# A new order for the first list of steps of a sparse-attention and gated-MLP kernel

## The chip, the cores and the metric

The kernel runs on one core of one Trainium2 chip. The metric is device time in microseconds for one execution, taken as the median of several runs. The kernel before takes 561.27 us (three runs, 560.92 to 561.34).

## The reference

Eight batches of 576 tokens. Each has eight heads of sparse attention: heads 0 to 3 look back within 32 tokens, heads 4 to 7 at the tokens of the same residue modulo 32. The heads' outputs, side by side, go through a gated MLP with a layer norm over half of its features, a mixing of tokens by `w_sg`, a projection and a residual. `w_in` and `w_out` come in float64.

```python
scores = scale * np.matmul(q, k.transpose(0, 1, 3, 2))
mask_local = (rel >= 0) & (rel < stride)
mask_strided = (rel >= 0) & (pos[None, :] % stride == pos[:, None] % stride)
...
attn = np.exp(scores)
attn = attn / (np.sum(attn, axis=-1, keepdims=True) + 1e-09)
return np.matmul(attn, v).astype(np.float32)
...
h = x @ w_in
h = 0.5 * h * (1.0 + np.tanh(c * (h + 0.044715 * h ** 3)))
u, v = (h[..., :d_ff // 2], h[..., d_ff // 2:])
v_n = (v - mu) / np.sqrt(var + 1e-06) * g_ln
v_s = np.einsum('ts,bsd->btd', w_sg, v_n) + b_sg[None, :, None]
return (x + (u * v_s) @ w_out).astype(np.float32)
```

## The kernel before

The work of a batch is cut into steps of one or a few instructions: a load (`qk_rows`, `v_load`), a block of matmuls (`local_scores`, `strided_pv`, `v_mm`, `u_mm`, `sg_mm`, `out_mm`), a softmax part (`sm_mask`, `sm_max`, `sm_sub`, `sm_exp`, `sm_sum`, `sm_mul`), a layer-norm part, a store. The table `STEPS` (line 978) gives each a short name, and four strings of such names, `START`, `SECOND`, `LATER` with `CYCLE`, and `LAST`, say in which order they are issued. `START` (line 25) is issued once, ahead of everything else: it holds all of the attention of batch 0, the attention of batch 1, the MLP of batch 0, and the preparation of the weights. The lists behind it go batch by batch, the attention of one batch woven into the MLP of the one before.

A word reads so: the name; `-` for the batch at hand, no sign for the next one (names in lower case: the batch at hand), `+` for the one after, `=` for a step of no batch; `^` sets a flag (line 1011) that moves the step to another place: with it `slow()` is VectorE instead of GpSimd, `fast()` is GpSimd instead of VectorE, loads go out on ScalarE's queue instead of SyncE's, and a PSUM tile comes from the other of two pools; behind `:` the number of a head pair, a tile or a weight piece. Every engine takes its instructions strictly in the order in which they are issued, and all DMA starts keep their order too (`InOrder`, line 72), so that an instruction that waits holds up all behind it on its engine.

The weights come in sixteen pieces (`halves`, line 268): eight of `w_in` (512 KB each, pieces 0 to 3 for v, 4 to 7 for u) and eight of `w_out` (256 KB each). Each is turned from the bits of float64 into a high and a low float32r part by a chain across engines: `cl` loads, `ck` clips a 16-bit field, `cc` combines it with the clip (VectorE, `scalar_tensor_tensor` with two SBUF operands), `ca` and `cd` scale on ScalarE, `ce` adds on GpSimd, `cg` copies the high part on ScalarE, `ch` subtracts for the low part on VectorE or GpSimd (tiles wil and wol). The same three-matmul scheme of high and low parts serves the activations: `x_high`, `x_low` (tile xt), `ln_high`, `ln_low` (vg, t1), `gate_high`, `gate_low` (vg again).

```python
def cv_signed(i):
    dve.scalar_tensor_tensor(
        ex.bitcast(F32), top, -18432.0, ex.bitcast(F32), op0=ALU.max, op1=ALU.subtract
    )
...
def gate_low(b, dc):
        fast().tensor_tensor(
            vg_tile()[:, dc, 1, cs], state[b, "gt", dc][:, lo:up], vg_tile()[:, dc, 0, cs], op=ALU.subtract
        )
```

Of batch 0 the local softmax runs in two parts (`sm_*` with 4 and 5, `PARTS`, line 557), so that it can start on the first four row blocks; `local_pt` and `local_pt_copy` turn P in the same two parts. `local_pv` (`VB`, line 681) is one step. `x_store` (`XR`) and `x_send` (`XD`) write the attention output to DRAM in four DMAs per head pair for the residual; their tile shares two buffers with the staged `w_sg` and the gates (tag gt).

Of the kernel before, what the change touches and what calls it, by code (L numbers as in the profile page):

```python
# [22 lines left out]


START = """
LP-:3 LP-:0 TP-:6 TP-^:7 TC-:7 wb= wc= TC-^:6 TP-^:0 mk= wd= ml=^ TC-:0 TP-^:1 LP-:1 cl=:0 mp= cl=:1 TC-:1 we=^
SS-^:3 SL-:0 cl=:8 cl=:2 MK-:3 MX-:3 cd=:0 TP-:3 SB-^:3 EX-:3 TP-^:2 MK-:4 TC-:3 TC-:2 wo= MX-:4 ck=:0 SB-^:4
cl=:9 ck=^:1 ck=:2 SL-^:1 LP-:2 cc=:1 SU-:3 cd=:1 ck=^:8 cc=:0 wl=:1 ML-^:3 TP-^:5 cd=^:8 ck=:9 cd=:9 mf= TP-:4
VT-^:0 ca=:0 LP:1 ca=:1 EX-:4 cd=:2 cc=:2 ca=:2 PS-:3 ce=:0 TC-:5 MK-:5 MX-:5 LP:0 cl=:3 TC-:4 cl=:5 SU-^:4
TP^:2 SS-^:2 SB-:5 EX-:5 cc=:8 SU-^:5 TC^:2 MK-^:2 CS-:3 cg=:0 cc=:9 wt=^:1 ce=:1 wp= ML-:4 MX-^:2 TP^:3 TC:3  # L30
ML-:5 PL-:5 ch=:0 PL-:4 SB-^:2 CL-:5 VT-:1 TP:0 wh=:1 EX-:2 LV-:0 CM-:5 CL-^:4 cg=:1 ce=:2 TP^:1 ck=:5 LV-:1
cd=:3 cg=:2 TC:0 wm=^:1 VB- SU-:2 ML-:2 ca=:8 cl=:7 cl=:4 ck=^:3 TC:1 ch=^:1 cc=:5 LV-:2 ck=^:7 XH-:1 SL^:0
ca=:9 ch=:2 cl=^:10 XH-:0 PS-:2 cc=:3 ca=:3 XR-:1 XL-:1 CS-:2 cc=:7 SL:1 ca=:7 XL-:0 LV-:3 PV-^:2 cd=:4 ce=:8
PW-:2 XR-:0 ck=^:4 va^:0 va:1 ce=:9 cd=:5 VT:0 cc=^:4 MK:0 XH-:2 MX:0 ce=:3 PV-:3 PW-^:3 SB^:0 ca=:4 XR-:2
XD-^:0 cd=:7 cl=:13 XL-:2 ce=:4 cg=:3 ce=:7 XH-^:3 ch=:3 cl=:6 cg=^:9 LP:3 ch=:9 cg=:4 XD-^:1 ck=:13 cd=:6 vb:1
vc:1 ck=^:6 lg= XL-:3 vb:0 ca=:5 vc:0 cg=:7 EX:0 LP:2 cc=:6 ce=:5 ch=^:4 ch=^:7 ca=:6 XD-^:2 vd:0 cg=:5 ce=:6
cc=:13 cd=:13 vd:1 g^:0 XR-:3 ca=:13 g:1 TP:6 SU:0 XD-^:3 LV:0 xt TP^:7 cg=:6 ch=^:5 LV:1 cg=:8 wl=:2 v^:2 wl=:4
ls:0 TP:4 cl=:11 ls:1 TC:7 ch=:6 lm:0 vh u^:0 TC:4 wl=:0 vl ce=:13 TP:5 u^:2 rt lr^:0 g:2 TC:5 ug:0 ls:2 wt=^:4
LQ+:0 lh:0 lm^:1 SS^:2 lm:2 VT:1 TC:6 ll:0 wl=:3 wh=:4 u^:1 wt=:0 lr:1 wm=:4 cd=:10 SS^:3 ck=^:10 lr:2 ug:2 MK:2
ug:1 wt=:2 cl=:15 cc=^:10 ML^:0 MK:3 ca=:10 u:3 ce=:10 LQ+:1 wh=:0 wh=:2 lh^:1 wm=:0 wm=:2 ll:1 ck=:11 cg=:10  # L40
ug:3 ch=:10 wt=^:3 wh=:3 lh:2 LV+:1 cl=:12 ck=:15 cg=:13 wm=:3 ll:2 PL:0 TQ+:0 cc=:15 cl=:14 s:1 cc=:11 cd=:11
sm:1 MX:3 s:0 CL:0 ca=:11 cd=:15 CM:0 MX:2 ca=:15 LQ+:3 SB^:3 ce=:11 ce=:15 VB LV+:0 sh:1 SB^:2 sm:0 EX:2 cg=:15
XH:0 cd=:12 sl:1 XR:1 ch=^:13 XH:1 LV:2 cg=^:11 ck=:14 cd=:14 ck=:12 ch=^:11 cc=:14 sh:0 cc=:12 s:2 EX:3 ca=:14
sl^:0 SU:2 ch=^:8 ce=:14 s:3 ca=:12 o:0 XL:1 ch=^:15 sm:2 ce=:12 XD:1 ML:2 SU:3 sh:2 sm:3 PS:2 CS:2 o^:1 cg=:12
XL:0 ML:3 cg=:14 PV:2 PW:2 o:2 r sh:3 sl^:2 XR:2 ch=^:12 sl:3 ch=:14 o2:2 TQ+^:1 os:2 LV^:3 o^:3 XR:0 XH:2 o2:3
os:3 o2^:0 od:2 os:0 o2:1 od^:3 od^:0 XL:2 os:1 od^:1 PS:3 CS:3 XD^:2 XD^:0 LQ+:2
"""
# [1014 lines left out]
```

## Time and profile before

| | |
|---|---|
| median of 3 runs | 561.27 us |
| the profiled execution | 561.67 us |
| its span, first to last instruction | 559.9 us |
| mean granted TensorE clock | 0.979 of 2.4 GHz |
| TensorE busy (matmul) | 531.0 us, 95% |
| VectorE busy | 408.5 us, 73% |
| ScalarE busy | 219.1 us, 39% |
| GpSimd busy | 192.3 us, 34% |
| chain that ended last | TensorE 82%, DMA 7%, VectorE 5% |

In the profile PE is TensorE's matmuls and PEld its weight loads, DVE is VectorE, ACT ScalarE, POOL GpSimd, and SP SyncE, which only issues DMAs here. Nearly every instruction is recorded by one helper, so the line is always L84, and instructions are told apart by the tiles that they write and read. A wait stands in brackets behind the instruction that waited, with what ended it.

### The profile page before, as it was taken

To read this page: it belongs to the slowest core of one execution; us is meant where nothing else is said; L and a number is where in the kernel's file an instruction comes from. 1 tells how busy PE (TensorE), PEld (TensorE's weight loads), DVE (VectorE), ACT (ScalarE), POOL (GpSimd) and SP (SyncE) were. 2 spreads that over 40 slices of the span, in tenths; PEclk is the share of its full clock that TensorE was granted. 3 is DMA by queue.
4 is the path that set the end of the run, shared out by engine and by line. 5 is a ranking of instruction groups with operands and counts; after the bars stand their busy time and mean duration, and the time that the engine had idled before them with its cause. 6 is when DMAs were issued, how large, how long until landed. Compare 5 with 4: busy or idle time off the path is not lost.

```text
span 559.9 us, 15951 instructions
## 1 busy us (share of the span) xinstructions
PE 531.0 (95%) x6705; PEld 476.8 (85%) x6705; DVE 408.5 (73%) x724; ACT 219.1 (39%) x365; POOL 192.3 (34%) x350
## 2 busy tenths in 40 slices
...
GB/s 191 236 219 162 195 141 109 167 108 101 103 89 124 177 112 69 104 133 179 47 88 126 152 131 76 88 142 175 50 88 124 166 141 2 24 117 129 2 0 95
DMA packets 235562, 65.56 MB, mean 117 GB/s; under 512 B 219681, under 2 KB 221217, under 8 KB 235490
## 3 DMA queue, kind: packets, MB, share of 16 engines
...
## 4 chain that ended last, share of the span: by engine, by line
PE 82%; DMA 7%; DVE 5%; SPq 2%; issue 1%; POOL 1%; ACT 1%; ACTq 0%; DVEq 0%; POOLq 0%
PE sg L84 19%; PE u L84 17%; PE o L84 17%; PE v L84 16%; DMA xd<-xs 2%; DMA rowk<-in_k_dram 2%; PE os L84 2%; SPq L84 2%; PE ss L84 2%; PE ol L84 2%; PE sa L84 2%; PE pts L84 2%; DMA stage<-in_moe_w_in_dram 1%; PE ptl L84 1%; DVE cv L84 1%
## 5 line engine op out<-in xcount | busy, mean ns | idle before, releaser
L84 PE MATMUL sg<-wsh,vg 128*128 128x288 f32 x512 | 113.5, 297 | 0.0
L84 PE MATMUL u<-xt,wih 128*128 128x288 f32 x512 | 103.5, 297 | 1.9 <-DVE hv L84 1.8
L84 PE MATMUL o<-woh,vg 128*128 128x512 f32 x288 | 96.1, 402 | 3.9 <-DVE gt L84 2.2
L84 PEld LDWEIGHTS sg<-wsh,vg 128*128 128x128 f32 x512 | 85.5, 188 | 0.3
L84 PEld LDWEIGHTS u<-xt,wih 128*128 128x128 f32 x512 | 81.8, 188 | 3.3 <-DVE hv L84 2.0
L84 PE MATMUL v<-wih,xt 128*128 128x512 f32 x256 | 83.0, 399 | 0.0
L84 PE MATMUL u<-xt,wil 128*128 128x288 f32 x256 | 75.6, 295 | 0.5 <-issue 0.5
L84 PE MATMUL sg<-wsl,vg 128*128 128x288 f32 x256 | 75.4, 294 | 0.0
L84 PEld LDWEIGHTS o<-woh,vg 128*128 128x128 f32 x288 | 54.5, 189 | 16.4 <-DVE ob L84 2.5
L84 DVE BATCH_NORM_STATS2 bnst<-hv 128x6 f32<-128x512 f32 (+1 forms) x40 | 27.0, 675 | 44.7 <-ACT hv L84 44.7
L84 PEld LDWEIGHTS v<-wih,xt 128*128 128x128 f32 x256 | 48.7, 190 | 10.6
L84 PE MATMUL o<-wol,vg 128*128 128x512 f32 x144 | 56.5, 392 | 0.0
L84 DVE TENSOR_TENSOR ob<-o,xn 128x512 f32<-128x512 f32 x32 | 20.9, 686 | 43.3 <-PE o L84 38.1
L84 PE MATMUL v<-wil,xt 128*128 128x512 f32 x128 | 50.6, 395 | 0.0
L84 PEld LDWEIGHTS u<-xt,wil 128*128 128x128 f32 x256 | 48.0, 188 | 0.7 <-issue 0.7
L84 PEld LDWEIGHTS sg<-wsl,vg 128*128 128x128 f32 x256 | 48.1, 188 | 0.0
L84 POOL CAST xtl<-xt 128x512 fp32r<-128x512 f32 x8 | 5.3, 668 | 104.4 <-DVE xt L84 104.4
L84 ACT COPY pts<-pts 128x576 f32<-128x576 f32 x16 | 10.2, 640 | 77.8 <-PE pts L84 68.0
L84 ACT CAST vg<-gt 128x576 fp32r<-128x576 f32 (+2 forms) x48 | 22.9, 512 | 44.5 <-DVE gt L84 41.1
L84 ACT ACTIVATE hv<-v 128x1024 f32<-128x1024 f32 x16 | 16.4, 1027 | 53.1 <-PE v L84 53.1
L84 POOL TENSOR_SCALAR va<-mv 128x2 f32<-128x2 f32 (+1 forms) x16 | 10.9, 680 | 74.8 <-DVE mv L84 74.7
L84 DVE TENSOR_TENSOR gt<-sg,u 128x576 f32<-128x576 f32 x32 | 23.7, 743 | 15.3 <-issue 7.5
...
## 6 DMA issues: line engine op xcount, KB each, us to landing
...
```

Source lines behind the costliest of these rows:

```text
L84: ins = self.tc.keep_in_program_order(op(*args, **kwargs))
```

## The change

The string `START` is written in a new order, and some steps get or lose `^`. Both orders have the same 393 words when `^` is left aside; 21 words differ in that sign, among them fifteen clips and low parts that change between VectorE and GpSimd in both directions, the subtractions `SB` of three softmax parts, `ML:3`, and `gate_low` of tiles 1 and 3, which go from VectorE to GpSimd. Nothing else in the file changes. The diff, cut:

```diff
-LP-:3 LP-:0 TP-:6 TP-^:7 TC-:7 wb= wc= TC-^:6 TP-^:0 mk= wd= ml=^ TC-:0 TP-^:1 LP-:1 cl=:0 mp= cl=:1 TC-:1 we=^
...
-ls:0 TP:4 cl=:11 ls:1 TC:7 ch=:6 lm:0 vh u^:0 TC:4 wl=:0 vl ce=:13 TP:5 u^:2 rt lr^:0 g:2 TC:5 ug:0 ls:2 wt=^:4
...
+LP-:3 mk= TP-:6 LP-:0 TP-^:7 TC-^:6 TC-:7 mp= TP-^:0 TC-:0 VT-^:0 ml=^ TP-^:1 cl=:1 SS-^:3 LP-:1 MK-:3 LP-:2
...
+wl=:2 cl=^:10 v^:2 wh=:4 TP:6 ls:0 u^:2 ck=:13 wm=:4 vh lr:1 TC:6 vl wl=:3 cc=:13 ug:2 cl=:11 LV:0 wt=:0 lm^:1
...
```

In engine order the change shows at three places. A row names the written tile and what it reads, with batch and buffer numbers; L84 is the helper's line.

The first place is VectorE around the first three subtractions into xt. cv is a piece of `w_in` under way, wil its low part, xs the store tile, ol and os the local and strided P V, sml the local scores of batch 1. Before:

```order
L84 TENSOR_TENSOR wil_90<-cv_1_316,wih_89 128x512
L84 SCALAR_TENSOR_TENSOR cv_5_573<-stage_102,cv_5_573 128x512
L84 TENSOR_SCALAR cv_7_641<-stage_102 128x512
L84 SCALAR_TENSOR_TENSOR cv_3_577<-stage_102,cv_3_577 128x512
L84 STREAM_TRANSPOSE xs_0_1_693<-ol_0_1_540 128x576
L84 TENSOR_TENSOR xt_97<-ol_0_1_540,xt_97 128x576
L84 SCALAR_TENSOR_TENSOR cv_7_641<-stage_102,cv_7_641 128x512
L84 TENSOR_TENSOR xt_97<-ol_0_0_400,xt_97 128x576
L84 STREAM_TRANSPOSE xs_0_0_781<-ol_0_0_400 128x576
```

Now, with the fourth subtraction at the end:

```order
L84 TENSOR_TENSOR wil_90<-cv_2_590,wih_89 128x512
L84 TENSOR_TENSOR wil_90<-cv_3_538,wih_89 128x512
L84 SCALAR_TENSOR_TENSOR cv_5_785<-stage_102,cv_5_785 128x512
L84 TENSOR_SCALAR cv_7_845<-stage_102 128x512
L84 TENSOR_TENSOR wol_92<-cx_316,woh_91 128x256
L84 SCALAR_TENSOR_TENSOR cv_6_822<-stage_102,cv_6_822 128x512
L84 SCALAR_TENSOR_TENSOR cv_7_845<-stage_102,cv_7_845 128x512
L84 TENSOR_SCALAR cv_4_904<-stage_102 128x512
L84 SCALAR_TENSOR_TENSOR cv_4_904<-stage_102,cv_4_904 128x512
L84 TENSOR_TENSOR xt_97<-os_0_2_765,xt_97 128x576
L84 STREAM_TRANSPOSE xs_0_2_919<-os_0_2_765 128x576
L84 TENSOR_TENSOR xt_97<-os_0_3_868,xt_97 128x576
```

The conversions of pieces 4 to 7 stood between the first and the third subtraction into xt; now they stand together, right ahead of the third and fourth, and xs of the third head pair stands between these two.

The second place is TensorE ahead of its first v matmul (v_0_0 and v_0_1 are the v tiles of batch 0, sa, sr and ss scores, pts the turned P of strided heads, turnq and turnk turned q and k of batch 1). Before:

```order
L84 MATMUL sa_1_644<-kT_1_0_634,qT_1_0_580 32x64 x32
L84 MATMUL pts_0_2_682<-ident_72,sms0_100 128x100 x8
L84 MATMUL sa_1_644<-kT_1_1_518,qT_1_1_492 32x64 x32
L84 MATMUL sr_1_699<-kT_1_0_634,qT_1_0_580 32x64 x2
L84 MATMUL sr_1_699<-kT_1_1_518,qT_1_1_492 32x64 x2
L84 MATMUL sr_1_699<-kT_1_0_634,qT_1_0_580 32x64 x2
L84 MATMUL sr_1_699<-kT_1_1_518,qT_1_1_492 32x64 x2
L84 MATMUL os_0_2_745<-pts_0_2_696,v_0_2_638 64x36 x32
L84 MATMUL v_0_0_784<-wih_89,xt_97 128x512
```

Now:

```order
L84 MATMUL pts_0_2_713<-ident_72,sms0_100 128x100 x8
L84 MATMUL turnk_1_2_725<-ident_72,rowk_1_2_588 128x96 x6
L84 MATMUL turnq_1_2_737<-ident_72,rowq_1_2_586 128x96 x6
L84 MATMUL v_0_1_749<-wih_89,xt_97 128x512
L84 MATMUL v_0_1_749<-wil_90,xt_97 128x512
L84 MATMUL v_0_1_749<-wih_89,xt_97 128x512 x2
L84 MATMUL v_0_1_749<-wil_90,xt_97 128x512
L84 MATMUL v_0_1_749<-wih_89,xt_97 128x512
L84 MATMUL pts_0_3_756<-ident_72,sms1_101 128x100 x8
L84 MATMUL os_0_2_765<-pts_0_2_723,v_0_2_493 64x36 x32
```

The v matmuls no longer stand behind P V of the third head pair; q and k of batch 1 are turned ahead of them.

The third place is GpSimd ahead of the out matmuls of batch 0 (vg from gt is `gate_low`, cxl a piece of `w_out`, wol its low part, sms a strided softmax). Before:

```order
L84 TENSOR_TENSOR vg_1122<-gt_0_0_1520,vg_1122 128x576
L84 TENSOR_TENSOR cxl_1221<-cxl_1221,cs_14_1385 128x256
L84 TENSOR_TENSOR cxl_1221<-cxl_1221,cs_12_1362 128x256
L84 TENSOR_TENSOR sms0_100<-sms0_100,sr_1_2_1574 100x16x36
L84 TENSOR_TENSOR sms1_101<-sms1_101,sr_1_3_1628 100x16x36
L84 TENSOR_TENSOR vg_1122<-gt_0_2_1619,vg_1122 128x576
L84 TENSOR_TENSOR wol_92<-cxl_1221,woh_91 128x256
```

Now:

```order
L84 TENSOR_TENSOR vg_1238<-gt_0_0_1464,vg_1238 128x576
L84 TENSOR_TENSOR sms0_100<-sms0_100,sr_1_2_1549 100x16x36
L84 TENSOR_TENSOR cxl_1286<-cxl_1286,cs_12_1340 128x256
L84 TENSOR_TENSOR cxl_1286<-cxl_1286,cs_14_1512 128x256
L84 TENSOR_TENSOR vg_1238<-gt_0_2_1643,vg_1238 128x576
L84 TENSOR_TENSOR vg_1238<-gt_0_3_1562,vg_1238 128x576
L84 TENSOR_TENSOR wol_92<-cxl_1286,woh_91 128x256 x2
```

The low part of gate 3 has come over from VectorE, and a softmax product (sms1) has gone the other way.

## Rows read from the trace of the kernel before

**Rows 1.** Busy time by stretch: length, then PE, PEld, DVE, ACT, POOL, clock, DMA, GB/s.

```profile
30.00:40.00 10.00, 6.88 (x101) 5.75 (x99) 9.41 (x16) 6.75 (x18) 6.73 (x6) 0.72 0.93 213
47.90:51.40 3.50, 3.50 (x10) 2.54 (x8) 3.36 (x5) 1.59 (x3) 2.85 (x3) 0.52 0.61 137
105.90:109.50 3.60, 3.60 (x15) 3.02 (x14) 0.90 (x4) 0.34 (x2) 2.52 (x2) 0.53 0.86 289
140.00:160.00 20.00, 20.00 (x269) 19.68 (x268) 19.38 (x34) 9.50 (x14) 9.92 (x18) 1.00 0.48 109
```

**Rows 2.** Timeline of TensorE: start, duration, instruction, idle time before and its releaser.

```profile
37.06 3.14 PE L84 MATMUL ol<-ptl,v_l 64*64 64x96 f32 x74 [0.15 <-DMA v_l<-in_v_dram]
...
46.05 1.14 PE L84 MATMUL os<-pts,v 36*64 36x36 f32 x64 [1.37 <-DVE xs L84]
47.12 0.50 PE L84 MATMUL v<-wih,xt 128*128 128x512 f32 x1
...
51.65 1.14 PE L84 MATMUL os<-pts,v 36*64 36x36 f32 x64
...
70.08 0.53 PE L84 MATMUL u<-xt,wih 128*128 128x288 f32 x2 [1.79 <-DVE hv L84]
...
85.86 0.38 PE L84 MATMUL sg<-wsh,vg 128*128 128x288 f32 x1
...
105.57 0.50 PE L84 MATMUL o<-woh,vg 128*128 128x512 f32 x1 [2.24 <-DVE gt L84]
...
115.86 0.50 PE L84 MATMUL o<-woh,vg 128*128 128x512 f32 x1 [0.91 <-DVE ob L84]
...
121.01 0.50 PE L84 MATMUL o<-woh,vg 128*128 128x512 f32 x1 [0.78 <-DVE ob L84]
```

**Rows 3.** VectorE by form, 10 to 110 us: busy us, mean ns, idle before.

```profile
L84 DVE SCALAR_TENSOR_TENSOR cv<-stage,cv 128x512 f32<-128x512 int16 x8 | 8.6, 1071 | 0.2
...
L84 DVE TENSOR_TENSOR wil<-cv,wih 128x512 fp32r<-128x512 f32 x4 | 5.9, 1501 | 0.0
L84 DVE SCALAR_TENSOR_TENSOR cx<-cs,cx 128x256 f32<-128x256 int16 x4 | 3.9, 979 | 0.0
...
L84 DVE SCALAR_TENSOR_TENSOR cxl<-cs,cxl 128x256 f32<-128x256 int16 x4 | 3.1, 784 | 0.4 <-POOL cxl L84 0.4
...
L84 DVE TENSOR_TENSOR sml<-sml,mx 128x1152 f32<-128x1152 f32 x1 | 2.3, 2256 | 0.0
...
L84 DVE TENSOR_TENSOR sml<-sml,sr 128x1152 f32<-128x1152 f32 x1 | 1.3, 1347 | 0.0
```

**Rows 4.** Timeline of VectorE, single steps.

```profile
17.75 0.69 DVE L84 SCALAR_TENSOR_TENSOR cv<-stage,cv 128x512 f32<-128x512 int16 x1
...
36.75 0.68 DVE L84 TENSOR_TENSOR wil<-cv,wih 128x512 fp32r<-128x512 f32 x1
37.58 2.87 DVE L84 SCALAR_TENSOR_TENSOR cv<-stage,cv 128x512 f32<-128x512 int16 x1
...
55.31 0.74 DVE L84 TENSOR_TENSOR xt<-os,xt 128x576 fp32r<-128x576 f32 x1
...
64.85 0.68 DVE L84 BATCH_NORM_STATS2 bnst<-hv 128x6 f32<-128x512 f32 x1
...
89.55 0.42 DVE L84 SCALAR_TENSOR_TENSOR cx<-cs,cx 128x256 f32<-128x256 int16 x1
```

**Rows 5.** Timeline of GpSimd around 38 us.

```profile
37.51 1.15 POOL L84 TENSOR_TENSOR sms<-sms,sr 100x576 f32<-100x576 f32 x1
38.62 1.27 POOL L84 TENSOR_TENSOR wil<-cv,wih 128x512 fp32r<-128x512 f32 x1
```

More of the change, by code (lines that the diff above doesn't have):

```diff
@@ L25 @@
 START = """
-LP-:3 LP-:0 TP-:6 TP-^:7 TC-:7 wb= wc= TC-^:6 TP-^:0 mk= wd= ml=^ TC-:0 TP-^:1 LP-:1 cl=:0 mp= cl=:1 TC-:1 we=^
[L27 to L35, printed above, removed]
@@ L36 @@
-vc:1 ck=^:6 lg= XL-:3 vb:0 ca=:5 vc:0 cg=:7 EX:0 LP:2 cc=:6 ce=:5 ch=^:4 ch=^:7 ca=:6 XD-^:2 vd:0 cg=:5 ce=:6
-cc=:13 cd=:13 vd:1 g^:0 XR-:3 ca=:13 g:1 TP:6 SU:0 XD-^:3 LV:0 xt TP^:7 cg=:6 ch=^:5 LV:1 cg=:8 wl=:2 v^:2 wl=:4
-ls:0 TP:4 cl=:11 ls:1 TC:7 ch=:6 lm:0 vh u^:0 TC:4 wl=:0 vl ce=:13 TP:5 u^:2 rt lr^:0 g:2 TC:5 ug:0 ls:2 wt=^:4
-LQ+:0 lh:0 lm^:1 SS^:2 lm:2 VT:1 TC:6 ll:0 wl=:3 wh=:4 u^:1 wt=:0 lr:1 wm=:4 cd=:10 SS^:3 ck=^:10 lr:2 ug:2 MK:2
-ug:1 wt=:2 cl=:15 cc=^:10 ML^:0 MK:3 ca=:10 u:3 ce=:10 LQ+:1 wh=:0 wh=:2 lh^:1 wm=:0 wm=:2 ll:1 ck=:11 cg=:10
@@ L41 @@
[L41 to L45, printed above, removed]
@@ L46 @@
-os:3 o2^:0 od:2 os:0 o2:1 od^:3 od^:0 XL:2 os:1 od^:1 PS:3 CS:3 XD^:2 XD^:0 LQ+:2
+LP-:3 mk= TP-:6 LP-:0 TP-^:7 TC-^:6 TC-:7 mp= TP-^:0 TC-:0 VT-^:0 ml=^ TP-^:1 cl=:1 SS-^:3 LP-:1 MK-:3 LP-:2
+cl=:9 TC-:1 SL-:0 cl=:8 MK-:4 cl=:0 ck=:1 MX-:4 TP-^:2 TP-:3 TC-:3 SB-:4 TC-:2 cd=:1 TP-:4 cc=:1 EX-:4 ck=:8
+TC-:4 MX-:3 wo= LP:1 SB-^:3 SU-^:4 SL-^:1 MK-:5 TP-^:5 ck=:9 VT:1 ca=:1 TP^:2 cd=:0 MX-:5 EX-:3 ck=^:0 SB-^:5
+ce=:1 TC-:5 LP:0 SS-^:2 cc=:0 cl=:3 wl=:1 TP^:3 EX-:5 SU-^:5 TC^:2 TP:0 ML-:5 wp= cl=:2 mf= MK-^:2 TC:3 cc=:9
@@ new lines @@
+LV-:0 SU-:3 LV-:2 ML-:4 TP^:1 PL-:5 ca=:0 TC:0 MX-^:2 LV-:1 LP:3 cd=:9 TC:1 CL-:5 wb= CM-:5 cd=:3 ML-^:3 ce=:0
+cc=:8 SB-^:2 SL^:0 EX-:2 wc= ck=^:3 VT-:1 PL-:4 LP:2 ck=^:2 SL:1 wt=^:1 cd=:2 cc=:3 SU-:2 cg=:1 CL-^:4 cc=:2
+ca=:2 cd=^:8 cl=:5 ML-:2 MK:0 wh=:1 ce=:2 cg=:0 wd= VB- MX:0 wm=^:1 ca=:3 XH-:0 PS-:2 ca=:9 CS-:2 TP:5 we=^
+ch=:0 ce=:3 VT:0 ce=:9 TP:4 TC:5 XL-:0 TC:4 va:1 PS-:3 PV-^:2 XR-:0 SB^:0 ck=:5 PW-:2 TP^:7 cl=:6 XH-:1 ca=:8
+cg=^:9 ch=^:1 cg=:2 XL-:1 CS-:3 cg=:3 XR-:1 cd=:6 va^:0 XH-:2 ch=^:2 ck=:6 cl=:7 ch=^:3 cl=:4 vb:1 cc=:5 ck=^:7
@@ new lines @@
+cd=:7 ch=^:9 LV-:3 cc=:6 vb:0 XD-^:0 cc=:7 EX:0 TC:7 PV-:3 ca=:7 ce=:7 ca=:6 PW-^:3 cd=:4 ce=:6 ck=^:4 XH-^:3
+cc=^:4 ca=:4 XL-:2 ce=:4 cd=:5 XD-^:1 cg=:7 XR-:2 XL-:3 vc:0 ce=:8 cg=:6 SU:0 ca=:5 XD-^:2 wl=:4 vc:1 lg= SS^:2
+vd:1 MK:2 xt cg=:4 g:1 ce=:5 LV:2 cg=:5 ch=:7 vd:0 cl=:13 XR-:3 ch=:5 ch=^:4 wl=:0 ch=:6 wt=^:4 XD-^:3 g^:0 ls:1
+wl=:2 cl=^:10 v^:2 wh=:4 TP:6 ls:0 u^:2 ck=:13 wm=:4 vh lr:1 TC:6 vl wl=:3 cc=:13 ug:2 cl=:11 LV:0 wt=:0 lm^:1
+wh=:0 g:2 lm:0 SS^:3 lr^:0 u^:1 cd=:13 ca=:13 ug:1 u:3 lh:0 wt=:2 ls:2 wm=:0 lh^:1 MK:3 ug:3 wh=:2 lm:2 ck=^:11
```

7 lines of the change are left out of this document (added).

## Prediction, made before the change was run

> **What bounds the kernel now.** I read the busy times by stretch first. From 140 us on TensorE is busy for the whole of each stretch: 20.00 of 20.00 us between 140 and 160 [rows 1], and the later stretches read alike. The change leaves everything behind the first list of steps as it was, so it can only move the moment at which that regime begins. What it can win lies in the first 125 us, and a microsecond won there arrives at the end undiminished, because TensorE is the bound from there on.
>
> Then I read TensorE's own timeline for its waits in that stretch [rows 2]. Three kinds stand there. In the first 46 us it waits for transfers and for small steps of other engines; the last of these waits are 0.15 us for v (start 37.06) and 1.37 us for VectorE's xs (start 46.05), after which the first v matmul begins at 47.12. In the middle there is one wait of 1.79 us ahead of u at 70.08. In the tail, ahead of o, there are 2.24, 0.91 and 0.78 us at 105.57, 115.86 and 121.01, all ended by VectorE: 3.93 us together. The clock adds to it: between 47.90 and 51.40 and between 105.90 and 109.50 the granted clock is 0.52 and 0.53, which is the 1.2 GHz level, with TensorE busy for all of both stretches [rows 1]; the second comes right behind the wait of 2.24 us.
>
> Then VectorE, which ends most of those waits. Its groups by form [rows 3] show one pattern: steps whose two big operands both lie in SBUF take far longer on average than a single one of them does elsewhere. `cv_signed` on 128x512 has a mean of 1071 ns over 8, and one of them takes 0.69 us at 17.75 [rows 4]; the subtraction into wil has 1501 ns over 4 against 0.68 us at 36.75; the 128x256 forms into cx and cxl have 979 and 784 ns against 0.42 us at 89.55; sml<-sml,mx takes 2256 ns where the product of the same shape, sml<-sml,sr, takes 1347. GpSimd's rows say why [rows 5]: the 2.87 us step of VectorE that starts at 37.58 [rows 4] ends at 40.45, about 0.6 us behind the second of two GpSimd steps on SBUF that run from 37.51 to 39.89. VectorE did not run slowly, it stood still.
>
> **What the change does to these terms.**
>
> *The price of the stretched steps.* Busy time less count times the single duration [rows 3, 4]: cv 8.6 - 8 x 0.69 = 3.1; wil 5.9 - 4 x 0.68 = 3.2; cx 3.9 - 4 x 0.42 = 2.2; cxl 3.1 - 4 x 0.42 = 1.4; sml 2.26 - 1.35 = 0.9. Together 10.8 us, of which all but the cxl share, 9.4 us, stands ahead of the first batch-norm step at 64.85. This is the most that keeping the two engines apart can give on VectorE.
>
> *The same work ahead of the gates.* A reordering helps only if it does not also put more work ahead of what TensorE needs. I compared the VectorE steps ahead of three gates in the two orders. Ahead of the first batch-norm step there are 87 instructions before and 84 now; the sets differ by eleven out and eight in, and at single durations that is 0.6 us less work. Ahead of the last subtraction of `ln_low`, on which sg waits, the sums differ by 0.7 us in the same direction. Ahead of the fourth xt subtraction (start 55.31) there are 2.1 us more, because four conversions were pulled forward. So the order by itself is about neutral; the gain has to come from the 9.4 us.
>
> *Term A, up to the batch-norm.* If VectorE never waited, the batch-norm could start 9.4 + 0.6 = 10.0 us sooner, at 54.9. It will wait, for data. By 37.06 us the queue had carried 7392 KB of loads, when TensorE got the last of v [rows 2]; the new order puts 7168 KB up to that point and 3488 KB more (q and k of the second batch, four halves of w_in, v of the fourth head pair) ahead of the fourth pair's P V. At the 213 GB/s of the stretch from 30 to 40 us [rows 1] the 3.57 MB take 16.8 us, so that P V can start near 36 + 16.8 = 53 us, against the 51.65 at which it ran before [rows 2]. The fourth xt subtraction then lands near 54.5 instead of 55.31 to 56.05, and behind it the new order has about 4.5 us of VectorE steps before the batch-norm: 59. I take **-6.0 us**, between 0 (loads bind throughout) and -10.0.
>
> *From there to sg.* VectorE's work between the two gates is the same within 0.1 us, and before it took 64.85 to 85.86, with the 1.79 us wait of TensorE inside. The lead is handed through: sg starts near 80.
>
> *Term C, the tail.* The 3.93 us of waits ahead of o and the clock behind the first of them (3.4 us at half speed, 1.7 us of work) are 5.6 us. The first wait goes to the PSUM bank of an sg tile that the next o tile takes over; the new order multiplies tile 3 first and multiplies the gate of tile 3 ten rows ahead of that of tile 2, so the bank should come free while tile 2 is still in the array. The two others wait for the PSUM of the earlier o, and the o steps still alternate between two tiles. I take half, **-2.8 us**, between 0 and -5.6.
>
> *Term D, new waits.* All four `gate_low` subtractions now stand on GpSimd, two of them in a row; two were VectorE's. XR of the third head pair now waits for the four sends of the first on VectorE's own queue, with the fourth xt subtraction behind it. I price this at one wait of the smallest kind seen, **+0.8 us** [rows 2], between 0 and +2.2. The other moved steps (mask building, the bias row, the late flags, the transposes of the third batch at the end) have TensorE's 46 us of loading or VectorE's emptier tail as cover, and I cost them nothing. That the local P V of the first batch comes in two parts costs nothing either: in both orders its 80 matmuls stand in one unbroken run, and what comes in two parts, its softmax and its P, did so before.
>
> *Sum.* -6.0 - 2.8 + 0.8 = -8.0 us. The profiled execution took 561.67 us, the median of the runs is 0.40 lower at 561.27, so the forecast is 553.3.
>
> **A rule against the trace.** The rows show VectorE standing through two GpSimd steps in a row [rows 4, 5], and the sum above takes the price of that meeting, 2.87 - 0.69 = 2.2 us, as it was measured. The Trainium skill ("SBUF — State Buffer", section "Who interferes with whom") says that VectorE and GpSimd share a port pair as an exclusive lock, held for one instruction, against which a VectorE step with two SBUF inputs stands while a GpSimd step reads SBUF. By that rule this step would have got in after the first of the two GpSimd steps, at 38.66, and ended near 39.4 instead of 40.45; 1.1 of the 9.4 us would not be there, and A could reach -8.9 at most instead of -10.0. The trace agrees that one stands for the other and disagrees on for how long; the measured price stays in the sum.
>
> **Rivals.**
> *The meetings move instead of vanishing.* For it: GpSimd's work is as much as before, VectorE with 9.41 busy of the 10 us from 30 to 40 [rows 1] has no gaps to dodge into, and engines drift against any plan as soon as one load is late. Against it: GpSimd is busy for only 6.73 of the same 10 us, so there is room. If half of the 9.4 us comes back, A is -1.3 and the time is 561.27 - 1.3 - 2.8 + 0.8 = 558.0. Chance 0.25.
> *The loads bind.* The fourth pair's P V slips by some 4 us more than I give it, A falls to -1, and TensorE reaches the tail as late as VectorE does, so half of C goes as well: 561.27 - 1.0 - 1.4 = 558.9. Chance 0.10.
> *Slower.* VectorE keeps all of its 9.4 us under the new order. Then the 2.1 us more work ahead of the fourth xt subtraction count in full, in front of the third and fourth pair's v matmuls, the tail gives nothing, and D stands: 561.27 + 2.1 + 0.8 = 564.2. Between this case (A +2.1) and the full gain (A -6.0) A grows with what is left of the stretching; with nothing from the tail it decides at A = -0.8, that is once some 6 of the 9.4 us are left. For it: an order cannot hold two engines apart, since neither waits for the other. Against it: what is pulled forward stood right behind the gate anyway. Chance 0.09.
> *Nothing to measure:* these cancel, within 0.2% (1.1 us, about what a measurement of this kernel can tell from no change). Chance 0.06.
>
> **The numbers.** The forecast has 0.50. With the first two rivals faster has 0.85, same 0.06, slower 0.09. The range goes from 549.0 (A -8 and C -4.2) to 560.0, which takes in both smaller gains; outside lie the slower case, the null and a sliver below, some 0.19.
>
> **What would show it.** Right: the wil and cv groups of VectorE come down to means near 0.7 us; the first v matmul some microseconds ahead of 47.12; the first batch-norm step near 59; sg near 80; the wait of 2.24 us ahead of o gone. Wrong: means above 1 us in those groups, a fourth xt subtraction later than 56, or a wait of several microseconds on VectorE's xs for the xd sends.

## The result and the profile after

The changed kernel takes 555.87 us (median of four runs, 555.47 to 556.34); the kernel before takes 561.20 in the runs beside it (560.92 to 561.34). The ratio is 0.9906, 95% interval 0.9889 to 0.9923: 5.3 us less, between 4.3 and 6.2. Forecast were 553.3 us and a range of 549.0 to 560.0. The time lies in that range, but the terms of the sum did not hold: the part that was to bring 6 us brought next to nothing, and the part that was to bring 2.8 brought nearly all there was.

The profiled execution took 556.34 us, its span is 554.3. First TensorE's timeline of the changed kernel (start, duration, instruction, idle time before and its releaser), the rows that answer to [rows 2]:

```profile
38.98 3.47 PE L84 MATMUL ol<-ptl,v_l 64*64 64x96 f32 x80 [2.69 <-DVE sml L84]
...
45.31 1.19 PE L84 MATMUL turnk<-ident,rowk 96*128 96x96 f32 x6 [1.33 <-DMA rowk<-in_k_dram]
...
47.28 0.80 PE L84 MATMUL v<-wih,xt 128*128 128x512 f32 x1
...
57.32 1.14 PE L84 MATMUL os<-pts,v 36*64 36x36 f32 x64
...
66.91 0.47 PE L84 MATMUL v<-wih,xtl 128*128 128x512 f32 x1 [0.83 <-ACT hv L84]
...
86.21 0.38 PE L84 MATMUL sg<-wsh,vg 128*128 128x288 f32 x1
...
117.74 0.50 PE L84 MATMUL v<-wih,xt 128*128 128x512 f32 x1 [0.64 <-DVE ob L84]
```

The first v matmul starts at 47.28 (47.12 before), sg at 86.21 (85.86 before): up to sg nothing is won. Behind it the waits of 2.24, 0.91 and 0.78 us ahead of o are gone; one of 0.64 us is left, ahead of the v matmul behind them.

VectorE by form, 10 to 110 us (busy us, mean ns, idle before), which answers to [rows 3]:

```profile
L84 DVE SCALAR_TENSOR_TENSOR cv<-stage,cv 128x512 f32<-128x512 int16 x8 | 5.6, 706 | 0.0
L84 DVE TENSOR_TENSOR wil<-cv,wih 128x512 fp32r<-128x512 f32 x4 | 3.0, 761 | 1.8 <-ACT wih L84 1.8
...
L84 DVE SCALAR_TENSOR_TENSOR cx<-cs,cx 128x256 f32<-128x256 int16 x4 | 1.7, 415 | 0.0
...
L84 DVE SCALAR_TENSOR_TENSOR cxl<-cs,cxl 128x256 f32<-128x256 int16 x4 | 1.6, 405 | 0.0
...
L84 DVE TENSOR_TENSOR sml<-sml,mx 128x1152 f32<-128x1152 f32 x1 | 1.3, 1316 | 0.0
```

Every one of the five groups is down to about the duration of a single undisturbed step: cv from 1071 to 706 ns, wil from 1501 to 761, cx from 979 to 415, cxl from 784 to 405, sml from 2256 to 1316. So the new order does hold the two engines apart, and of the 10.8 us that the prediction counted some 10.6 are back: 8.6 + 5.9 + 3.9 + 3.1 + 2.3 = 23.8 us of busy time before, 13.2 now.

Where did they go? Busy time by stretch (length, PE, PEld, DVE, ACT, POOL, clock, DMA, GB/s), first the changed kernel, then the kernel before, whose row for 30 to 40 us is in [rows 1]:

```profile
30.00:40.00 10.00, 4.62 (x142) 3.53 (x137) 8.19 (x21) 6.30 (x16) 3.55 (x3) 0.72 1.08 206
40.00:50.00 10.00, 8.67 (x92) 7.49 (x85) 6.56 (x10) 5.78 (x11) 5.91 (x5) 0.50 1.06 214
50.00:60.00 10.00, 10.00 (x168) 8.40 (x167) 7.41 (x14) 7.63 (x13) 4.72 (x4) 0.93 0.67 118
```

```profile
40.00:50.00 10.00, 7.44 (x227) 5.90 (x227) 9.80 (x16) 6.65 (x12) 5.04 (x5) 0.84 0.55 126
50.00:60.00 10.00, 10.00 (x101) 8.00 (x100) 8.74 (x9) 6.63 (x11) 8.85 (x7) 0.93 0.96 213
```

From 30 to 60 us VectorE was busy for 9.41 + 9.80 + 8.74 = 27.95 us and is now for 8.19 + 6.56 + 7.41 = 22.16: 5.8 us less busy time, and as much more idle time. The largest waits of VectorE in that stretch (who waited, for whom, us, times, longest), after and then before:

```profile
DVE xt L84 <- ACT xt L84: 4.2, 3, 2.4
DVE wil L84 <- ACT wih L84: 1.8, 1, 1.8
DVE cv L84 <- DMA stage<-in_moe_w_in_dram: 1.3, 1, 1.3
```

```profile
DVE cv L84 <- DMA stage<-in_moe_w_in_dram: 1.2, 1, 1.2
```

And the chain of waits, as the profile infers it, tells what they wait for in the end. Pieces of it from 27 us on (start, duration, what), before and then after:

```profile
27.62 7.47 DMA stage<-in_moe_w_in_dram
...
35.59 1.96 POOL cv L84
...
37.58 2.43 DVE cv L84
```

```profile
27.47 9.04 DMA v<-in_v_dram
...
36.57 8.60 DMA rowk<-in_k_dram
...
45.31 1.19 PE turnk L84 x6
```

Before, the chain ran from a load through GpSimd's clip into the 2.87 us step of [rows 4] and on through VectorE's steps. Now it runs from load to load: v, then k of batch 1's third head pair, which lands at 45.17; its turn stands ahead of the first v matmul.

The gain is in the tail. Busy time from 85 to 125 us, before and then after:

```profile
85.00:95.00 10.00, 9.78 (x121) 9.37 (x121) 8.68 (x16) 7.12 (x16) 4.00 (x4) 1.00 0.44 89
95.00:105.00 10.00, 8.33 (x96) 8.02 (x85) 8.63 (x15) 5.18 (x12) 6.38 (x6) 1.00 0.77 158
105.00:115.00 10.00, 9.38 (x96) 7.33 (x96) 5.90 (x11) 3.14 (x6) 3.25 (x3) 0.83 0.51 153
115.00:125.00 10.00, 8.36 (x40) 6.67 (x41) 4.22 (x7) 0.64 (x1) 0.00 (x0) 1.00 0.29 106
```

```profile
85.00:95.00 10.00, 10.00 (x128) 9.73 (x131) 9.54 (x19) 8.32 (x19) 3.30 (x4) 1.00 0.52 118
95.00:105.00 10.00, 10.00 (x102) 9.74 (x91) 6.81 (x17) 3.91 (x8) 5.86 (x6) 1.00 0.84 194
105.00:115.00 10.00, 10.00 (x108) 7.93 (x107) 6.47 (x11) 3.60 (x8) 5.26 (x5) 1.00 0.73 177
115.00:125.00 10.00, 9.37 (x100) 7.32 (x99) 4.17 (x7) 1.92 (x2) 0.61 (x1) 1.00 0.76 161
```

TensorE was busy for 35.85 of these 40 us, with a mean clock of 0.83 in one of the four stretches, which is 10 x 0.17 = 1.7 us of work lost; now it is busy for 39.37 at a clock of 1.00. That is 3.5 + 1.7 = 5.2 us, about the whole of the measured gain.

### The profile page after: what moved, and what is told of

It is laid out like the page before. It is cut to its first block, busy times and chain, and to the rows that moved or that the text cites. A ratio compares the mean times of both kernels' runs of the same rounds, so it can differ in the third digit from the quotient of the medians.

```text
span 554.3 us, 15949 instructions
## 1 busy us (share of the span) xinstructions
PE 531.3 (96%) x6705; PEld 477.3 (86%) x6705; DVE 396.4 (72%) x725; ACT 219.6 (40%) x365; POOL 190.2 (34%) x349
## 4 chain that ended last, share of the span: by engine, by line
PE 83%; DVE 6%; DMA 6%; SPq 3%; issue 1%; ACT 1%; DVEq 0%
PE sg L84 19%; PE v L84 18%; PE o L84 17%; PE u L84 16%; DMA rowk<-in_k_dram 3%; PE os L84 3%; SPq L84 3%; PE ol L84 2%; PE pts L84 2%; PE ss L84 2%; DMA v<-in_v_dram 2%; PE sa L84 1%; PE ptl L84 1%; DVE sr L84 1%; DVE hv L84 1%
## 5 line engine op out<-in xcount | busy, mean ns | idle before, releaser
L84 PE MATMUL sg<-wsh,vg 128*128 128x288 f32 x512 | 113.5, 297 | 0.0
L84 PE MATMUL u<-xt,wih 128*128 128x288 f32 x512 | 103.5, 297 | 0.0
L84 PE MATMUL o<-woh,vg 128*128 128x512 f32 x288 | 94.7, 398 | 0.0
L84 PEld LDWEIGHTS sg<-wsh,vg 128*128 128x128 f32 x512 | 85.6, 188 | 0.3
L84 PE MATMUL v<-wih,xt 128*128 128x512 f32 x256 | 83.5, 399 | 0.6 <-DVE ob L84 0.6
L84 PEld LDWEIGHTS u<-xt,wih 128*128 128x128 f32 x512 | 81.7, 188 | 1.2
L84 PE MATMUL u<-xt,wil 128*128 128x288 f32 x256 | 75.4, 295 | 0.0
L84 PE MATMUL sg<-wsl,vg 128*128 128x288 f32 x256 | 75.4, 294 | 0.0
L84 PEld LDWEIGHTS o<-woh,vg 128*128 128x128 f32 x288 | 54.1, 188 | 11.2
L84 DVE BATCH_NORM_STATS2 bnst<-hv 128x6 f32<-128x512 f32 (+1 forms) x40 | 27.0, 675 | 44.7 <-ACT hv L84 44.7
L84 PEld LDWEIGHTS v<-wih,xt 128*128 128x128 f32 x256 | 48.6, 190 | 11.6 <-DVE ob L84 1.1
L84 PE MATMUL o<-wol,vg 128*128 128x512 f32 x144 | 56.2, 390 | 0.0
L84 DVE TENSOR_TENSOR ob<-o,xn 128x512 f32<-128x512 f32 x32 | 20.9, 687 | 42.1 <-PE o L84 40.7
L84 PE MATMUL v<-wil,xt 128*128 128x512 f32 x128 | 50.3, 393 | 0.0
L84 PEld LDWEIGHTS sg<-wsl,vg 128*128 128x128 f32 x256 | 48.1, 188 | 0.0
L84 PEld LDWEIGHTS u<-xt,wil 128*128 128x128 f32 x256 | 48.0, 188 | 0.0
L84 POOL CAST xtl<-xt 128x512 fp32r<-128x512 f32 x8 | 4.9, 610 | 100.0 <-DVE xt L84 100.0
L84 ACT CAST vg<-gt 128x576 fp32r<-128x576 f32 (+2 forms) x48 | 22.8, 512 | 40.9 <-DVE gt L84 40.7
L84 ACT ACTIVATE hv<-v 128x1024 f32<-128x1024 f32 x16 | 16.4, 1028 | 53.8 <-PE v L84 53.8
L84 ACT COPY pts<-pts 128x576 f32<-128x576 f32 x16 | 10.2, 640 | 67.1 <-PE pts L84 67.1
L84 POOL TENSOR_SCALAR va<-mv 128x2 f32<-128x2 f32 (+1 forms) x16 | 10.1, 629 | 72.2 <-DVE mv L84 71.9
L84 DVE TENSOR_TENSOR gt<-sg,u 128x576 f32<-128x576 f32 x32 | 23.7, 742 | 13.1 <-issue 7.5
```

The lines of the kernel that those rows point to most:

```text
L84: ins = self.tc.keep_in_program_order(op(*args, **kwargs))
```

## The experiments

Two questions stood: why 10 us of VectorE's stalls were worth nothing in the front (up to sg), and what made the tail faster. Times are given as the ratio to the kernel before on the same chip, times 561.27 us; in brackets the 95% interval. The changed kernel itself stands at -5.3 (-6.2 to -4.3). A row of an experiment names line 83 where before and after have 84.

### Front and tail apart

The list is cut ahead of the first sg block of the old order. The first kernel has the 296 words ahead of the cut in the new order and with the new signs, and the rest as it was:

```diff
-LP-:3 LP-:0 TP-:6 TP-^:7
+LP-:3 mk= TP-:6 LP-:0
...
-cg=:13 wm=:3 ll:2 PL:0 TQ+:0 cc=:15 cl=:14
+cc=:15 cl=:14 ch=^:10 TQ+:0 rt
 s:1 cc=:11 cd=:11 sm:1 MX:3 s:0 CL:0
```

> The 296 steps that the old order has ahead of its first sg block, in the new order and on the new engines; the rest as before. Theory 1 (all of the gain lies behind the first sg matmul, since the traces show the same work done by 100 us in both): 560.5 to 562. Theory 2 (the front is worth the 6 us of the prediction and something else hid it): 555 to 556. In either case the wil and cv groups of VectorE come down to means near 0.75 us. If theory 1 holds, the 2.24 us wait ahead of o is there again.

Measured: ratio 1.019 (1.0157 to 1.0222), 10.7 us slower. Neither theory had that. VectorE's wil and cv groups do come down to 678 and 676 ns, and sg starts at 85.53. Behind it, the old tail does not fit: the loads of `w_out` come late, and the wait ahead of o grows. A row of VectorE and one of TensorE:

```profile
92.54 0.29 DVE L83 TENSOR_SCALAR cxl<-cs 128x256 f32<-128x256 int16 x1 [4.61 <-DMA cs<-in_moe_w_out_dram]
...
115.03 0.79 PE L83 MATMUL o<-woh,vg 128*128 128x512 f32 x1 [6.32 <-DVE gt L83]
```

The total therefore says nothing of the front, but the time of sg does: 85.53 against 85.86 before and 86.21 with all of the change. In a single profile that is no difference: the old front ran twice more, in two kernels below that differ from the kernel before only behind it, and there sg starts at 86.89 (new tail) and 85.93 (two o words swapped). So one front scatters by 1 us at sg, and the new front is worth nothing that can be told from that. This run also bears on a rival that came up with the result: in the changed kernel TensorE runs at half clock (0.50) all through 40 to 50 us, so the clock could have eaten the gain. Here the same front had a higher clock in 40 to 45 and 45 to 47 us:

```profile
40.00:45.00 5.00, 3.72 (x78) 3.41 (x74) 3.49 (x7) 2.63 (x5) 3.61 (x3) 0.69 1.07 212
45.00:47.00 2.00, 1.11 (x10) 1.14 (x11) 1.56 (x2) 0.33 (x1) 0.00 (x0) 0.87 1.01 240
```

and sg came 0.7 us earlier than with the clock at 0.50, which is again within that scatter. A bound comes from the changed kernel's own rows: from its first v matmul to sg the mean clock is 0.95, so 38.93 x 0.05 = 1.9 us went to the clock, and the two turns ahead of it, 2.0 us at half clock, hold another 1.0. By this estimate a full clock could have given some 3 us in the front, not six. No run tried it.

The second kernel is the mirror: the old front, then the new tail.

```diff
 wm=:3 ll:2 PL:0 TQ+:0 cc=:15 cl=:14
-s:1 cc=:11 cd=:11 sm:1 MX:3 s:0 CL:0
+LV:2 cc=:11 ca=:11 cd=:11 CL:0 ce=:11 MX:2 MX:3 SB:2 EX:2 s:1 s:0 CM:0
...
-r sh:3 sl^:2 XR:2 ch=^:12 sl:3
+sh:3 sl^:2 XL:0 sl^:3 ch=:14 XR:2
```

> The mirror of the one before: the first 296 steps as before, the rest in the new order and on the new engines. Theory 1: 555.5 to 557, and the wil group stays near 1.5 us on VectorE. Theory 2: 558 to 559 (the tail's 2.8 us alone).

Measured: ratio 0.9939 (0.9913 to 0.9965), -3.4 us (-4.9 to -2.0), between the two forecasts, with parts of both inside the interval. All of TensorE's waits from 95 to 135 us:

```profile
96.38 1.73 PE L83 MATMUL ol<-ptl,v_l 64*64 64x96 f32 x78 [0.99 <-ACT ptl L83]
108.73 0.50 PE L83 MATMUL o<-woh,vg 128*128 128x512 f32 x1 [0.23 <-DVE gt L83]
120.47 0.50 PE L83 MATMUL v<-wih,xt 128*128 128x512 f32 x1 [0.57 <-DVE ob L83]
```

The wait of 2.24 us ahead of the first o is gone (it starts at 106.20), one of 0.23 us stands ahead of a later o, and the two for ob ahead of o are gone. But a new one of 0.99 us stands ahead of P V of batch 1: ten steps that the new order issues ahead of sg, among them the copy of the turned P (CL:0) that this matmul waits for, come behind the cut here. From sg to the second P V behind the first o it is 40.21 us before (85.86 to 126.07), 36.53 here (86.89 to 123.42) and 34.47 in the changed kernel (86.21 to 120.68). So most of the gain needs only the new tail; the rest, some 2 us, comes with a front that does those ten steps.

### The price of the stalls, with the order unchanged

GpSimd's work is cut down in place, in the old order and in the new:

```diff
-        pool.tensor_tensor(ex, ex, mid, op=ALU.add)
+        pool.tensor_tensor(ex[:, 0:32], ex[:, 0:32], mid[:, 0:32], op=ALU.add)
...
+        if b < 2 and not alt[0]:
+            view, ngrp = view[:, 0:1], 1
```

> The kernel before with GpSimd's work cut down where that can be done in place: cv_add on 32 of its 512 or 256 columns, and the GpSimd softmax subtractions and products of batches 0 and 1 on one group; the order, VectorE's steps and the loads are the same. It leaves out most of these additions, subtractions and products. Theory A (the stretched VectorE steps hold TensorE up in the front, as the prediction has it): wil and cv means near 0.7 us and the time near 553 to 555. Theory B (in the front transfers and the work between engines set the pace; the stretched steps cost TensorE only in the tail): means near 0.7 us and 558 to 560, with sg starting within 1.5 us of 85.86 and the 2.24 us wait ahead of o gone.

> The changed kernel with the same cut, which leaves out the same work. Both theories: little is left to take away, 554.5 to 556. Below 553: GpSimd's own pace, not its meetings with VectorE, holds the changed kernel.

Measured: the old order 0.997 (0.9946 to 0.9995), -1.7 us (-3.0 to -0.3); the new order 0.9914 (0.9889 to 0.9939), which is +0.4 against the changed kernel, with an interval of about 1.7 us to both sides. The old order under the cut, two of VectorE's groups from 10 to 70 us and two rows of TensorE:

```profile
L83 DVE SCALAR_TENSOR_TENSOR cv<-stage,cv 128x512 f32<-128x512 int16 x8 | 5.8, 726 | 0.1
L83 DVE TENSOR_TENSOR wil<-cv,wih 128x512 fp32r<-128x512 f32 x4 | 2.9, 725 | 0.0
```

```profile
85.28 0.38 PE L83 MATMUL sg<-wsh,vg 128*128 128x288 f32 x1
...
103.89 0.50 PE L83 MATMUL o<-woh,vg 128*128 128x512 f32 x1 [1.14 <-DVE gt L83]
```

This is the experiment that decides on the prediction's main term. The stalls of the front are gone with the order as it was, VectorE has most of its time back, and sg starts only 0.6 us earlier (85.28 for 85.86). The ten executions together gain 1.7 us and at most 3.0, and in the profile 2.4 of the gain lie behind sg (37.83 us from there to the second P V behind the first o, 40.21 before). Theory A, that these stalls hold TensorE up by some 6 us, falls.

But these 0.6 us, within the scatter of sg, are not all that the stalls cost. VectorE is 2.0 us ahead in this profile (its second xs ends at 43.96 instead of 45.95), and TensorE does not make use of it. It waits 2.90 us, for nothing that the profile shows, up to 42.77; from there to sg it has no wait, and it runs at half clock where the kernel before, with its waits, had the full one. Busy time from 44 to 48 us, before and then here:

```profile
44.00:48.00 4.00, 2.16 (x69) 1.81 (x69) 3.90 (x8) 2.50 (x5) 0.04 (x1) 1.00 0.28 58
44.00:48.00 4.00, 4.00 (x140) 3.40 (x141) 2.49 (x7) 2.28 (x4) 0.00 (x0) 0.50 0.50 95
```

So the first v matmul comes at 48.51, 1.4 us later than before, and the 1.79 us wait ahead of u is gone: from the first v matmul to sg TensorE takes 36.77 us, which is its busy time in the same stretch before. With VectorE's stalls gone the next limit is TensorE itself, and its clock.

In the tail the first wait halves, from 2.24 to 1.14 us. In the kernel before it came behind a meeting of VectorE with GpSimd's `gate_low`, which ran from 99.93 to 101.36:

```profile
99.99 1.66 DVE L84 SCALAR_TENSOR_TENSOR cxl<-cs,cxl 128x256 f32<-128x256 int16 x1 [0.41 <-POOL cxl L84]
```

The thinned kernel still has this one, which may be why the wait does not vanish: its cxl step takes 1.65 us, from 99.09 on, while `gate_low`, which was not cut, runs from 99.02 to 100.46.

### What else holds the front: the loads

Half of the bytes of w_in are left unloaded, in the new order and in the old:

```diff
+    for j in (1, 0, 2, 3, 4):
+        dve.memset(stage[64:128, j], 0)
...
-            for a in range(2):
+            for a in range(1):
...
-            loads().dma_start(dst, halves[i][0].bitcast(I16))
+            m = 64 if i < 8 else P
+            loads().dma_start(dst[0:m], halves[i][0][0:m].bitcast(I16))
```

> The changed kernel with half of the bytes of w_in's eight pieces (256 of 512 KB each; partitions 64 to 127 are set to zero once at the start on VectorE, which is idle there, and not loaded). It leaves out the loading of half of w_in; every step is there. Ahead of the transfer that the turn in front of the first v matmul waits for (landing at 45.2) that is 1 MB less, 4.9 us at 213 GB/s. If loads set the front of the changed kernel: first v near 43 instead of 47.28, sg near 82, and 551 to 553. If not: 555 to 556.

> The kernel before with the same half of w_in left unloaded. If in the old order the stretched VectorE steps set the front and loads only the little behind: 560 to 561.5, and the gap to the changed kernel under the same cut grows from 5.3 to 8 us or more. If loads set the front of both: it gains as the changed kernel does, 556 to 558, and the gap stays near 5.

Measured: the new order 0.9815 (0.9778 to 0.9851), which is 550.9 us and 5.1 less than the changed kernel, with some 2.3 us to both sides. Its profiled execution took 557.92 us, longer than the changed kernel, so its rows cannot show where the gain arises. The old order 0.9994 (0.9976 to 1.0013): no gain at all. The gap between the orders grows from 5.3 to 10 us. Rows of TensorE in the old order, and VectorE's wil group:

```profile
41.98 0.49 PE L83 MATMUL sr<-kT,qT 64*32 64x64 f32 x16 [2.41 <-DVE xt L83]
44.59 1.94 PE L83 MATMUL os<-pts,v 36*64 36x36 f32 x64 [2.13 <-DVE xs L83]
...
46.46 0.79 PE L83 MATMUL v<-wih,xt 128*128 128x512 f32 x1
```

```profile
L83 DVE TENSOR_TENSOR wil<-cv,wih 128x512 fp32r<-128x512 f32 x4 | 7.7, 1956 | 0.0
```

With its loads halved the old order starts local P V at 33.92 instead of 35.88 and then waits twice for VectorE, 2.41 and 2.13 us; wil is stretched even more. The two pairs together bear on the front so. Take away the stalls alone, and the time falls by 1.7 us, most of it in the tail; take away loads alone, and it does not move; take away both, and it falls by another 5.1 us. That fits two limits that end close together, of which the change removed one. The old front points the same way without any cut: in the two kernels that repeat it the first v matmul starts at 49.34 and 48.74 instead of 47.12, the wait ahead of u shrinks from 1.79 to 0.25 us in both, and sg stays within 1.0 us of 85.86.

It is not shown that the 5.1 us arise in the front. The profile that there is has neither of the two milestones that were expected: the first v matmul starts at 45.69 and not near 43, behind a turn that still waits 1.33 us for its load, and sg starts at 88.26 and not near 82, with a mean clock of 0.86 between the two (0.95 in the changed kernel).

### VectorE work put back

```diff
+        if i < 8:
+            seen = p1.tile([P, 1], F32, tag="seen", name="seen", bufs=1)
+            dve.tensor_reduce(seen, ex.bitcast(F32), axis=AX.X, op=ALU.max)
         dve.scalar_tensor_tensor(
```

> The kernel before with one more VectorE step ahead of each of the eight cv_signed of w_in: a maximum over ex, 128x512, some 0.69 us each (as the reduction over 128x512), 5.5 us in all, its result unused. If VectorE's own work sets the front of the kernel before: 561.2 + 5.5 = 566.7. If transfers set it and VectorE only ends last by little: 561.2 to 563.

> The changed kernel with the same eight steps. If VectorE now waits for transfers in the front, it takes up part of the 5.5 us in its idle time: 556 to 558. If VectorE's work still sets the front: 555.9 + 5.5 = 561.4.

Measured: the old order 1.0042 (1.0023 to 1.0061), +2.4 us; the new order 0.9982 (0.9963 to 1.0001), +4.3 against the changed kernel. Neither came out in either of its two cases; the new order came nearer to the one in which VectorE's work still counts. In the old order part of the 5.5 us was paid by fewer meetings: cv went from 1071 to 924 ns and wil from 1501 to 1394, 8 x 0.147 + 4 x 0.107 = 1.6 us. In the new order VectorE waits in some places and not in others: the extra steps ahead of cv stand where it does not, right ahead of the mask that frees P V's PSUM (that wait grows from 2.69 to 3.96 us) and of the third xt subtraction, where TensorE now waits:

```profile
62.34 1.22 PE L83 MATMUL v<-wih,xt 128*128 128x512 f32 x2 [2.41 <-DVE xt L83]
```

Idle time of an engine, added up over a stretch, is not slack for a step at a given place.

### Single waits of the changed kernel

Three edits went at single waits in the new front. Turning q and k of the third head pair later, out of the way of the first v matmul:

```diff
-CS-:2 TP:5 we=^ ch=:0 ce=:3 VT:0 ce=:9 TP:4 TC:5 XL-:0 TC:4 va:1
+CS-:2 we=^ ch=:0 ce=:3 VT:0 ce=:9 XL-:0 va:1
...
-vb:1 cc=:5
+vb:1 TP:5 TP:4 TC:5 TC:4 cc=:5
```

> The changed kernel with four words moved: q and k of batch 1's third head pair are turned (TP:5 TP:4 TC:5 TC:4) behind the second v block of tile 1 (vb:1) instead of ahead of the first v matmul. In the changed kernel the first v matmul stands behind a turn that waits 1.33 us for its transfer and starts at 47.28. If that place in TensorE's order costs the front its gain: first v near 44.5 and 553.5 to 554.9. If other waits take its place: first v earlier, sg near 86 all the same, and 555.5 to 556.5.

Measured: 1.0023 (0.999 to 1.0056), 6.6 us slower than the changed kernel, which neither case had. The first v matmul starts at 43.89, 3.4 us earlier, and then the turn itself waits:

```profile
58.01 1.20 PE L83 MATMUL turnk<-ident,rowk 96*128 96x96 f32 x6 [6.83 <-issue]
```

The profile names nothing that it waits for. It starts 0.1 us after VectorE's xs of the third pair ends (57.91), so the likely reason is that the turned k now takes the PSUM tile of that pair's P V, which xs frees; and xs stands behind four conversions that came late with their loads.

Loading and converting the first two pieces of `w_out` later:

```diff
-cl=:9 TC-:1 SL-:0 cl=:8 MK-:4
+TC-:1 SL-:0 MK-:4
...
-cl=:4 vb:1
+cl=:4 cl=:9 cl=:8 vb:1
...
-ck=^:4 XH-^:3
+ck=^:4 ck=:8 ck=:9 cc=:9 cd=:9 cc=:8 cd=^:8 ca=:9 ce=:9 ca=:8 cg=^:9 XH-^:3
```

> The changed kernel with the first two pieces of w_out (8 and 9; 512 KB) loaded and converted behind w_in's instead of ahead of most of it. If the amount of loads ahead of P V sets the front: 512 KB at 213 GB/s are 2.4 us, local P V starts near 36.6 instead of 38.98 and the time is 553.5 to 554.5. If not: 555.5 to 556.5, or later if the two pieces now meet the tail.

Measured: 0.9972 (0.995 to 0.9994), 3.7 us slower than the changed kernel. P V does start earlier, at 36.73, and the turn of k at 44.23 instead of 45.31, so 512 KB are worth 1 to 2 us there; then the moved conversions stand ahead of the third xt subtraction, and TensorE waits for it:

```profile
62.43 1.22 PE L83 MATMUL v<-wih,xt 128*128 128x512 f32 x2 [3.56 <-DVE xt L83]
```

Masking batch 1's local scores earlier, so that P V gets its PSUM:

```diff
-LP:2 ck=^:2 SL:1 wt=^:1 cd=:2
+LP:2 ck=^:2 SL:1 MK:0 wt=^:1 cd=:2
...
-cl=:5 ML-:2 MK:0 wh=:1
+cl=:5 ML-:2 wh=:1
```

> The changed kernel with one word moved: the masking of batch 1's local scores (MK:0), whose PSUM the local P V of batch 0 waits 2.69 us for, stands right behind the scores (SL:1), ahead of two cv_signed that wait for loads. P V starts near 37 instead of 38.98. If loads set the first v matmul: the wait for rowk ahead of it grows by as much as P V gains, and the time stays at 555.5 to 556.5. If P V's start sets it: 553.5 to 554.5.

Measured: 0.9882 (0.9859 to 0.9905), -1.3 against the changed kernel with 1.6 to both sides: not told apart. TensorE's rows:

```profile
38.27 0.59 PE L83 MATMUL ol<-ptl,v_l 64*64 64x96 f32 x6 [0.95 <-DVE sml L83]
39.20 3.14 PE L83 MATMUL ol<-ptl,v_l 64*64 64x96 f32 x74 [0.33 <-DMA v_l<-in_v_dram]
```

P V wins 0.7 us and not 2; the wait for v_l is next in line, and the turn, at 44.95, still waits 1.09 us for its load.

### The order of the o tiles

```diff
-CS:2 o^:1 cg=:12 XL:0 ML:3 cg=:14 PV:2 PW:2 o:2
+CS:2 o:2 cg=:12 XL:0 ML:3 cg=:14 PV:2 PW:2 o^:1
```

> The kernel before with two words swapped: the first half of out tile 2 ahead of that of tile 1 (o:2 and o^:1), as in the new order, so that two o tiles in a row come from the same PSUM pool. If the order of the o tiles made the waits of 0.91 and 0.78 us ahead of o: both gone, 559.5 to 560.5. If they come from VectorE being late with ob: they stay, 561 to 561.5.

Measured: 1.0062 (1.0042 to 1.0083), 3.5 us slower, and the waits stay:

```profile
110.18 0.79 PE L83 MATMUL o<-woh,vg 128*128 128x512 f32 x1 [1.31 <-DVE gt L83]
118.28 0.50 PE L83 MATMUL o<-woh,vg 128*128 128x512 f32 x1 [0.86 <-DVE ob L83]
```

This swap by itself is no gain; it even adds a wait for the next gate, of which the new tail, where the gates are multiplied earlier, has at most 0.23 us (in the second kernel above).

It does not reach the two waits that it aimed at. Out tiles 0 and 1, and 2 and 3, are halves of one PSUM tile (`out_mm`), and the old list puts the next matmuls into such a tile right behind the step that reads it: `os:2 LV^:3 o^:3` and `os:0 o2:1`, with the two transposes of `TQ+^:1` on VectorE ahead of `os:2`. In the rows these are the two waits: VectorE's ob ends at 115.80 and 120.96, and TensorE goes on at 115.86 and 121.01. The new list puts six matmuls of the other tile in between (`os:2 o2^:0 o^:3`, `os:0 o2:3 od^:0 o2:1`) and `TQ+^:1` well ahead; there ob ends at 112.37, while TensorE is still in these matmuls. Every kernel here with the new tail is without the two waits, and every one with the old tail has them. That these words alone do it was not tested.

## Why the prediction was right in its sum and wrong in its terms

The forecast of 553.3 us missed the measured 555.87 by 2.6 us, and that it came so near is luck in part: term A was some 6 us too good, and terms C and D together some 3 us too bad.

**What bounds the kernel** held: what was won ahead of 125 us arrived at the end, 5.2 us of TensorE's time for 5.3 measured.

**The stretched steps** held: 10.8 us were counted, 10.6 came back, and every group fell to about the duration that the prediction had for one step (wil, the farthest off, to 761 ns for 680).

**Term A, -6.0 up to the batch-norm, is the step that failed.** The first batch-norm step starts at 65.74 where 59 was forecast and 64.85 stood before; the fourth pair's P V at 57.32 where 53 was forecast; sg at 86.21 where 80 was. The runs show two mistakes in it. First, it priced VectorE's stalls and set the loads against the fourth P V alone, while in the new order a load already holds the first v matmul: it lands at 45.17, and from its turn to 57.32 TensorE had no wait at all. With GpSimd thinned out the old order lost the same stalls and gained 1.7 us in all; in its profile sg came 0.6 us earlier. Second, it was never set against TensorE's own timeline. Between its first v matmul and sg TensorE waited only 1.79 us before [rows 2], and lost 1.7 to the clock: with the first v matmul where it was, no relief of VectorE could be worth more than 3.5 us. Of these 2.7 are still there, a wait of 0.83 us and 1.9 us lost to the clock (0.50 from 47.28 to about 51). The rest went into work: TensorE now does 460 matmuls between the two, where it did 403, P V of the third pair among them, and is busy for 38.10 us instead of 36.77. The rival in which the loads bind named this front (a fourth P V some 4 us later than 53, A near -1), and its time missed mainly because it halved the tail as well.

The prediction had shown in the second place of the order that q and k of batch 1 are turned ahead of the first v matmul, and gave that no price. That turn waits 1.33 us. Moved behind the v matmuls it cost more than it gave, as the run with the later turn shows.

**Term C, -2.8 for the tail, was right in kind and half of its size**: 5.2 us, against an upper end of 5.6. The reason that it gave for the first wait fits the rows: the gate of tile 3 is multiplied from 99.57 on, and the first o, at 103.65, comes right behind the matmuls ahead of it. It took half because the waits for ob seemed to be tied to the PSUM of the earlier o; they are, but it did not see that the new list puts another tile's matmuls in between. It also left out that the stretching of the tail sat in front of the first o: the thinned GpSimd halves that wait with the order unchanged, and with it goes the stretch at half clock behind it. The new tail on the old front has -3.4 of the gain. What is left comes with ten steps that the new order does ahead of sg, which would mean that the time that VectorE won in the front was spent in part on the tail's work. That share, some 2 us, comes from a difference of two runs and was not tested by itself.

**Term D, +0.8, came to nothing**: no wait for the sends of the first pair stands ahead of the third xs, and no wait of TensorE in the tail names GpSimd, which now does the four `gate_low` steps (the first o matmul, at 103.65, has no wait).

**The rule against the trace.** The run with the thinned GpSimd repeats the comparison with "SBUF — State Buffer" of the Trainium skill (section "Who interferes with whom"), by which VectorE stands for one GpSimd instruction: there VectorE's cxl step ends 0.28 us behind `gate_low`, though GpSimd goes straight on to its next step; by that rule, the trace agrees here. For the step that stood through two GpSimd steps [rows 4, 5] it does not, and why stays open.
